# Writing out TensorE's order and the engine of each flexible task as two strings, in place of rules that decide them while the program is built

## The chip, the cores and the metric

The kernel runs on one core of one Trainium2 chip. The metric is device time in microseconds; the time before is the median of three runs. A core has a matrix engine (TensorE, PE in the profile; its weight loads are PEld), a vector engine (VectorE, DVE), a scalar engine (ScalarE, ACT), GpSimd (POOL) and SyncE (SP), which here issues DMAs. Each engine works off its own list of instructions in order; semaphores hold it where an input isn't there yet. TensorE writes to PSUM, and VectorE or ScalarE carry the result to SBUF (an eviction).

## The reference, cut to what matters

B is 8, S 3136, D 256 and d_qk 64; all inputs are float32.

```python
scores = (1 / S) * np.matmul(z, z.transpose(0, 2, 1))
attn = np.maximum(scores, 0.0) ** 2
x = u * np.matmul(attn, v)                       # stage 1
proj = x @ w_proj                                # stage 2
x1, x2, x3 = proj[..., :D], proj[..., D:2*D], proj[..., 2*D:]
x2_conv = irfft(rfft(x2, axis=1) * rfft(filter_fft, axis=0), axis=1)
out = (x1 * x2_conv * x3) @ w_out
```

## The kernel before

**Stage 1.** A batch's 3136 rows are cut into seven chunks of columns (CHUNKS: five of 512, one of 256, one of 320) and 25 tiles of 128 rows. A unit is a pair of row tiles against one chunk. Its scores (`score_mm`, task kind S) contract over only 64 rows, so the array is used in halves (64x128) or, next to spectrum work, in quarters (64x64). Relu runs on ScalarE from PSUM into R_t (line 1852), the square on VectorE (line 1861) or ScalarE (line 1859) into A_t in bf16, and the product with v (`weigh`, kind W, full array) sums into the two PSUM banks ps_o. As the scores are symmetric, some squares are transposed by DMA into the tiles M_t, M2e_t and M2o_t and used a second time. When a chunk is complete, VectorE multiplies the sum by the transposed u into xT_t (line 1903).

**Stage 2.** `add_proj` projects each finished chunk (kind A, in the last batch partly Z): gates x1*x3 (line 1217), and x2 through the first step of a Fourier transform written as matmuls (`dft1`), whose result goes to a scratch in DRAM (s_t to spec). When a batch's scratch is complete, `add_spectrum` loads it and runs the quarter-array steps forward and inverse (kind Q), with the multiplication by the filter's transform H on VectorE between (line 1307); the result goes to a second scratch. `add_end` (kind B, or Z for chunks that are put back to the end) loads that, finishes the transform, multiplies by the gates (line 1401), applies w_out and stores.

**PSUM.** Two banks hold the sums ps_o; six banks form three pairs ps_s. S and Q take a whole pair, A, B and Z one bank of a pair, of which at most three may be held at a time.

**The planner.** The program's order is not the order in which the Python code is written. Every piece of work is a `Task` with its cost on each engine that may run it, its dependencies and the buffers it takes. `Plan.go` steps through a clock of its own: it asks `pick_pe` for TensorE's next task and `pick` for each other engine's, takes the one that can begin first and emits its instructions. TensorE's tasks wait in queues by kind (S, Q, W, FA, FB, FZ); S and W leave theirs in order, Q within the first four, the F kinds within the first six. `pick_pe` chooses the kind by rules: stay with S while it is in a run of them, how much W must be in hand, whether a Q joins the run, a credit that balances W against projections. The numbers of the rules stand in RULES, one line for each 50 us of the planner's clock. Tasks that may run on either of two engines (evictions by `copy`, squares) are offered to both, and `pick` gives a task to its second engine only if it would end earlier there, with a term `give` for tasks that can't move. `fill` puts a matmul of the identity on TensorE where it would be idle near the end.

The relus run on ScalarE alone, the products with gates and with H on VectorE alone. Three queues issue DMAs: SyncE (scratch, transposes, stores), GpSimd (loads with a cast, some stores), and ScalarE (a few at the very start and end).

Of the kernel before, what the change touches and what calls it, by code (L numbers as in the profile page):

```python
# [37 lines left out]
MOST = 3  # L38
REACH = 2
Rule = namedtuple("Rule", "backlog ample stay first lead pace full give")  # L40
STEP = 50.0
RULES = [
    Rule(1.25, 5.0, 0.05, 0.5, 1, 0.5, 3.0, 1.0),
    Rule(1.25, 5.0, 0.05, 0.5, 1, 0.5, 3.0, 1.0),
    Rule(1.25, 5.0, 0.05, 0.5, 1, 0.45, 3.0, 1.0),
    Rule(1.25, 5.0, 0.05, 0.5, 1, 0.45, 3.0, 1.0),
    Rule(1.25, 5.0, 0.05, 0.5, 1, 0.45, 3.0, 1.0),
    Rule(1.25, 5.0, 0.05, 0.5, 1, 0.5, 3.0, 1.0),
    Rule(1.25, 5.0, 0.05, 0, 1, 0.55, 3.0, 1.0),
    Rule(1.25, 5.0, 0.05, 0.5, 1, 0.5, 3.0, 1.0),  # L50
    Rule(1.25, 5.0, 0.05, 0.5, 1, 0.5, 3.0, 1.0),
    Rule(1.25, 6.0, 0.05, 0.5, 1, 0.5, 3.0, 1.0),
    Rule(1.25, 6.0, 0.05, 0.5, 1, 0.5, 3.0, 1.0),
    Rule(1.25, 5.0, 0.05, 0.5, 1, 0.5, 3.0, 1.0),
    Rule(0.5, 6.0, 0.05, 0, 0, 0.4, 99, 0.5),
    Rule(0.5, 6.0, 0.05, 0, 0, 0.4, 99, 0.5),
    Rule(0.5, 6.0, 0.05, 0, 0, 0.4, 99, 0.5),
    Rule(1.25, 5.0, 0.1, 1, 1, 0.5, 3.5, 1.0),
    Rule(1.75, 99.0, 0.3, 0.5, 1, 0.55, 4.0, 1.0),
    Rule(1.25, 5.0, 0.05, 0.5, 1, 0.5, 3.0, 0),  # L60
    Rule(1.25, 5.0, 0.3, 0.5, 1, 0.6, 3.0, 1.0),
    Rule(1.25, 5.0, 0.05, 0.5, 1, 0.5, 3.0, 0),
]
SHARE = {0: 1, 2: 3}

# [117 lines left out]
class Task:  # L183


    def __init__(self, emit, cost, deps=(), takes=(), prio=0, lat=None, moves=0.0, late=0.0):
        self.emit, self.cost, self.takes, self.prio = emit, cost, list(takes), prio
        self.lat, self.moves, self.late = lat, moves, late
        self.deps = [d if isinstance(d, tuple) else (d, None) for d in deps]
        self.kids, self.frees = [], []  # L190
        self.left = len(self.deps)
        self.ready = 0.0
        self.end = None
        self.holders = 1
        for d, _ in self.deps:
            d.kids.append(self)
# [9 lines left out]
class Plan:  # L206


    def __init__(self):
# [3 lines left out]
        self.credit = 0.0  # L213
        self.mode = None
        self.quarters = False
        self.quad_run = self.score_run = 0
        self.soon = False
        self.n = 0
# [4 lines left out]
    def add(self, task, kind=None):  # L223
        task.kind = kind
        task.no = self.n
        self.n += 1
        if kind:
# [56 lines left out]
    def backlog(self):  # L284
        left = 0.0
        for w in self.queues["W"]:
            if w.source is not None and w.source.end is None:
                break
            left += w.cost["PE"]
        return left  # L290

    def queued(self, t):
        some = {id(x): x for e in ("ACT", "DVE") for x in self.pend[e] if x.ready <= t + 0.3}
        return sum(max(0.0, self.free[e] - t) for e in ("ACT", "DVE")) + sum(min(x.cost.values()) for x in some.values())

    def rule(self, t):
        return RULES[min(int(t / STEP), len(RULES) - 1)]

    def pick_pe(self):
        t = self.free["PE"]  # L300
        now = self.rule(t)
        got = {}
        for k, window in (("S", 1), ("Q", 4), ("W", 1), ("FA", 6), ("FB", 6), ("FZ", 6)):
            best = None
            for task in self.queues[k][:window]:
                s = max(t, self.ready_at(task))
                if s < INF and (best is None or s < best[0] - 1e-9):
                    best = (s, task)
            if best:
                got[k] = best  # L310
        if not got:
            return None
        more = self.queues["S"]
        quad = got.pop("Q", None)
        if self.mode == "S" and self.quarters and quad and quad[0] <= t + now.stay:
            if not more or self.quad_run < 1 and self.score_run >= now.lead:
                return (*quad, "Q")
        if more and not more[0].left:
            left = self.backlog()
            if self.mode == "S":  # L320
                if "S" in got and got["S"][0] <= t + now.stay:
                    return (*got["S"], "S")
                got.pop("S", None)
                if self.quarters and quad and quad[0] <= t + now.stay and self.quad_run < 1:
                    return (*quad, "Q")
            else:
                want = 3 if left > now.ample else 2
                free = self.pairs.when(min(want, len(more)) - 1)
                first = quad and quad[0] <= t + 0.3 and left > now.first
                if "S" in got and free > t + 0.04:  # L330
                    rest = {k: v for k, v in got.items() if k != "S" and (k == "W" or left > now.backlog)}
                    if rest and min(v[0] for v in rest.values()) < free:
                        got = rest
                    elif free < INF:
                        if first and not now.lead:
                            return max(quad[0], free), quad[1], "Q"
                        self.soon = bool(first)
                        return max(got["S"][0], free), got["S"][1], "S"
                elif "S" in got:
                    if first and not now.lead:  # L340
                        return (*quad, "Q")
                    self.soon = bool(first)
        elif quad:
            got["Q"] = quad
        if not got and quad:
            return (*quad, "Q")
        if not got:
            return None
        near = t + 0.04
        order = ["S", "Q"]  # L350
        order += ["FA", "FB", "W", "FZ"] if self.credit > 0 and self.queued(t) < now.full else ["W", "FA", "FB", "FZ"]
        for k in order:
            if k in got and got[k][0] <= near:
                return (*got[k], k)
        k = min(got, key=lambda k: (got[k][0], order.index(k)))
        return (*got[k], k)

    def pick(self, e):
        t = self.free[e]
        best = None  # L360
        for task in self.pend[e]:
            s = max(t, self.ready_at(task))
            if s == INF:
                continue
            first = next(iter(task.cost))
            if e != first:
                behind = sum(
                    x.cost[first] for x in self.pend[first]
                    if x is not task and x.prio <= task.prio and next(iter(x.cost)) == first and x.ready <= s + 0.3
                )  # L370
                end = s + task.cost[e]
                held = max((end - max(x.ready, s) for x in self.pend[e] if len(x.cost) == 1 and x.ready < end), default=0.0)
                if end + self.rule(t).give * held >= max(self.free[first], task.ready) + behind + task.cost[first]:
                    continue
            key = (round(s / 0.03), task.prio, task.no)
            if best is None or key < best[0]:
# [17 lines left out]
    def go(self):  # L394
        while True:
# [13 lines left out]
            if k:  # L409
                self.queues[k].remove(task)  # L410
                half = k in ("S", "Q")
                if half != (self.mode == "S") and self.mode:
                    start += 0.096
                    self.quarters, self.quad_run, self.score_run = half and self.soon, 0, 0
                self.score_run += k == "S"
                if k == "Q":
                    self.quad_run += 1
                    if self.score_run and not self.quarters:
                        start += 0.092
                    self.quarters = True  # L420
                self.mode = "S" if half else k
                if k == "W":
                    self.credit = min(self.credit + self.rule(start).pace, 2.0)
                elif k != "S":
                    self.credit = max(self.credit - task.cost["PE"], -2.0)
            self.run(task, e, start)
        left = sum(len(q) for q in self.queues.values()) + sum(len(q) for q in self.pend.values())
# [4 lines left out]
def kernel(  # L432
# [838 lines left out]
    def add_spectrum(b, puts, early=0):  # L1271
# [5 lines left out]
        homes = [l_p, l_p, gs_p, gs_p]  # L1277
        lasts = []
        behind = []
        ldb, gb = [None], [None]  # L1280
        for g in range(NJ // 2):
# [4 lines left out]
            if g % 2 == 0 and final:  # L1286
                ldb[0] = load_parts(D1[b % 2], 2 * g, 4, puts[:early], puts[early:], homes[g // 2])
# [709 lines left out]
```

## Time and profile before

| | |
|---|---|
| median of 3 runs | 985.75 us (985.3 to 986.08) |
| span of the profiled execution | 983.6 us |
| VectorE, multiplication by H, 120 of 128x1024 bf16 | 82.3 us |
| PE weight loads from v_t, 128x128, 2706 | 243.0 us |
| SyncE's hardware queue (q1), share of 16 DMA engines | 63.1% |
| GpSimd's software queue (q0), share of 16 DMA engines | 23.7% |
| HBM read and written | 90.26 MB and 53.35 MB |

The profiled execution's own time is its span; the runs are measured from outside and come out some 2 us longer. In a row of a group stand line, engine, operation, output and input tiles, shapes and count, then busy time, the mean of one in ns, and the idle time of the engine ahead of them with what ended it. In a row of the timeline stand start, duration, engine, line, operation and count, neighbours of one kind merged. A busy TensorE is not one at its peak: matmuls overlap, and their ends are modelled.

### The profile page before, as it was taken

The numbers are of one execution on the slowest core, as the hardware profiler recorded it, in microseconds if no ns is written. First come the engines' busy times: TensorE is split into PE (matmuls) and PEld (weight loads), VectorE is DVE, ScalarE is ACT, GpSimd is POOL, SyncE is SP. The second block draws the span as 40 slices with busy tenths as digits, with TensorE's granted clock in tenths as the row PEclk, the third lists the DMA queues.
The fourth block names the chain that finished last, engine by engine and source line by source line (L and its number), as shares of the span: only waits on it lengthen the run. The fifth ranks groups of instructions, "written<-read, shape, count | busy, mean of one in ns | idle before, by whom it ended". The sixth has DMA issues, their size and how long they took to land.

```text
span 983.6 us, 19551 instructions
## 1 busy us (share of the span) xinstructions
PE 946.7 (96%) x6776; PEld 470.0 (48%) x6877; DVE 832.4 (85%) x1468; ACT 855.6 (87%) x1185; POOL 204.4 (21%) x426
## 2 busy tenths in 40 slices
PE   6999999999999999999999999999999999999986
PEld 2344544455544544445444454544544454544654
DVE  8966798998788887988879998799788997888885
ACT  5988898899888998899988899799988999999773
POOL 5142311222022301213111230113202222000040
PEclk9999999999999999999999999999999999999999
DMA  9799789979899689997699888997869978896677
GB/s 166 140 175 160 144 144 172 180 131 162 179 216 187 128 159 203 192 184 144 143 210 197 167 153 175 209 192 151 157 158 205 215 137 146 178 221 135 172 209 227
DMA packets 332403, 170.32 MB, mean 173 GB/s; under 512 B 242598, under 2 KB 307942, under 8 KB 332304
## 3 DMA queue, kind: packets, MB, share of 16 engines
q1 hardware_dynamic: 302496, 132.43, 63.1%
q0 software_dynamic: 29168, 35.13, 23.7%
q10 hardware_dynamic: 640, 1.51, 0.5%
q8 instruction: 54, 0.88, 0.4%
q14 instruction: 45, 0.37, 0.1%
HBM read 90.26 MB, written 53.35 MB: 146 GB/s over the span
## 4 chain that ended last, share of the span: by engine, by line
PE 77%; DVE 10%; ACT 5%; issue 5%; DMA 1%; ACTq 0%; POOL 0%; DVEq 0%; SPq 0%; POOLq 0%
PE ps_o_t L561 45%; PE ps_s L561 32%; DVE A_t L1861 4%; ACT R_t L1852 3%; DVE xT_t L1903 1%; DVE xh L1307 1%; DVE gate_t L1217 1%; DVE yT_t L1401 1%; ACT A_t L1859 1%; DMA spec<-s_t 0%; ACT x_t L594 0%; DVE gs_t L598 0%; ACT s_t L594 0%; DMA spec<-gs_t 0%; DMA zn_t<-in_z_dram 0%
## 5 line engine op out<-in xcount | busy, mean ns | idle before, releaser
L1852 ACT ACTIVATE R_t<-ps_s 128x1024 f32<-128x1024 f32 (+4 forms) x512 | 467.0, 965 | 71.2 <-PE ps_s L561 68.0
L561 PE MATMUL ps_o_t<-A_t,v_t 128*128 128x512 bf16 (+4 forms) x2009 | 447.5, 353 | 9.7 <-issue 4.8
L1861 DVE TENSOR_TENSOR A_t<-R_t 128x1024 bf16<-128x1024 f32 (+3 forms) x311 | 342.8, 1119 | 58.9 <-ACT R_t L1852 58.3
L561 PEld LDWEIGHTS <-v_t 128*128 128x128 bf16 (+2 forms) x2870 | 249.0, 98 | 259.8 <-issue 74.5
L1859 ACT ACTIVATE A_t<-R_t 128x1024 bf16<-128x1024 f32 (+4 forms) x185 | 186.5, 1018 | 1.2
L561 PE MATMUL ps_s<-zT_t 64*128 64x512 bf16 (+4 forms) x1512 | 169.9, 357 | 1.6 <-DVE zT_t L598 0.5
L644 POOL COPY tick<-xT_t 1x1 bf16<-1x1 bf16 x54 | 17.9, 331 | 693.7 <-DVE xT_t L1903 693.7
L561 PE MATMUL ps_s<-xT_t,wp 128*128 128x512 bf16 (+2 forms) x412 | 101.1, 351 | 3.6 <-ACT R_t L1852 0.9
L561 PEld LDWEIGHTS <-zT_t 64*64 64x64 bf16 (+1 forms) x1545 | 52.6, 101 | 101.7 <-issue 85.8
L594 ACT ACTIVATE x_t<-ps_s 128x512 bf16<-128x512 f32 (+2 forms) x152 | 82.2, 583 | 16.0 <-PE ps_s L561 12.1
L1903 DVE SCALAR_TENSOR_TENSOR xT_t<-ps_o_t,uT_t 128x256 bf16<-128x256 f32 (+2 forms) x224 | 76.1, 383 | 10.8 <-PE ps_o_t L561 8.6
L1307 DVE TENSOR_TENSOR xh<-xh,H 128x1024 bf16<-128x1024 bf16 x120 | 82.3, 686 | 0.8
L561 PE MATMUL ps_o_t<-M_t,v_t 128*128 128x512 bf16 (+2 forms) x352 | 81.8, 353 | 0.0
L1217 DVE TENSOR_TENSOR gate_t<-ps_s,x_t 128x256 bf16<-128x256 f32 (+2 forms) x214 | 71.0, 384 | 12.5 <-PE ps_s L561 10.7
L1401 DVE TENSOR_TENSOR yT_t<-ps_s,gate_t 128x512 bf16<-128x512 f32 (+2 forms) x98 | 58.4, 626 | 11.1 <-PE ps_s L561 10.1
L561 PEld LDWEIGHTS <-wp 128*128 128x128 bf16 x448 | 42.6, 98 | 45.6 <-issue 10.3
L635 POOL DMA_DIRECT2D un_t<-in_u_dram x112 | 60.1, 561 | 5.3 <-issue 4.5
L654 POOL DMA_DIRECT2D v_t<-in_v_dram x112 | 59.6, 557 | 4.8 <-DMA v_t<-in_v_dram 1.9
L598 DVE CAST xh<-ps_s 128x512 bf16<-128x512 f32 x62 | 41.8, 687 | 18.6 <-PE ps_s L561 17.7
L561 PE MATMUL ps_s<-wp,xT_t 128*128 128x256 bf16 x398 | 56.6, 273 | 0.2
L561 PE MATMUL ps_s<-wo,yT_t 128*128 128x256 bf16 (+1 forms) x338 | 49.8, 273 | 0.7 <-ACT R_t L1852 0.4
L594 ACT ACTIVATE s_t<-ps_s 128x512 bf16<-128x512 f32 (+1 forms) x82 | 46.9, 593 | 1.8 <-issue 0.9
(165 smaller groups left out, 840.9 us busy)
## 6 DMA issues: line engine op xcount, KB each, us to landing
out_dram<-ost_t SPq DMA_DIRECT2D x60, 256.0 KB
spec<-s_t SPq DMA_DIRECT2D x96, 128.0 KB
spec_in_t<-spec SPq DMA_DIRECT2D x56, 192.0 KB
spec<-gs_t SPq DMA_DIRECT2D x56, 192.0 KB
v_t<-in_v_dram POOLq DMA_DIRECT2D x80, 128.0 KB, 4.8
un_t<-in_u_dram POOLq DMA_DIRECT2D x80, 128.0 KB, 5.4
conv_in_t<-spec SPq DMA_DIRECT2D x34, 256.0 KB
out_dram<-ost_t SPq DMA_DIRECT2D x18, 128.0 KB
```

Of the source, the lines that this page charges most:

```text
L561: wrote(nc.tensor.matmul(o, *args, **kw), o)
L594: got = nc.scalar.activation(out_, in_, AF.Copy)
L598: got = nc.vector.tensor_copy(out_, in_)
L635: nc.gpsimd.dma_start(out=t[ds(j * N1, N1), lo - t0 : hi - t0, :], in_=x[:, n2 : n2 + hi - lo, :])
L654: nc.gpsimd.dma_start(out=t[ds(j * N1, N1), ds(v_at(a), (b - a) * D)], in_=r[:, n2 + a - lo : n2 + b - lo, :].rearrange("p t d -> p (t d)"),)
L1217: got = nc.vector.tensor_tensor(g[:, ::-1] if h == 0 else g, p, x, ALU.mult)
L1307: nc.vector.tensor_tensor(x[:, 1 - i], x[:, 0], h, ALU.mult)
L1401: got = nc.vector.tensor_tensor(yb["y"][:, dh, 0:w], p, gates[b, c, dh][:, 0:w], ALU.mult)
L1852: has_read(nc.scalar.activation(blocks(box["R"], n, cw)[:rows], p, AF.Relu), p)
L1859: nc.scalar.activation(a, r, AF.Square)
L1861: nc.vector.tensor_tensor(a, r, r, ALU.mult)
L1903: nc.vector.scalar_tensor_tensor(x, f, inv_s2, ut, ALU.mult, ALU.mult)
```

## The change

RULES, the functions that read them (`backlog`, `queued`, `rule`) and the choices in `pick_pe` and `pick` go. Two strings take their place. ORDER has one letter for each task of TensorE: `pick_pe` takes the next letter and then, within that kind's queue, the task that can begin first; TensorE waits for it even if another kind could begin. ENGINES has one letter (a for ScalarE, d for VectorE) for each task that may run on either engine, in the order in which the tasks are created; `go` strikes the other engine from the task before the clock starts. When each engine's tasks run is still decided by the planner's clock. `fill` stays. Whether a run of S and Q uses quarters is now read ahead in the string.

Beside this a weight task may be split by rows and run on the half array (letters w and v, functions `weigh_rows`, `by_rows` and the task `second`); ORDER has neither letter. `weigh_short` goes through `by_rows`, which adds a wait only when the rows of one sum change; in `weigh_short` they don't. In the last batch the two spectrum loads that go into gs buffers also wait until the last inverse of the batch before has been issued (`after_q`).

```diff
-RULES = [
-    Rule(1.25, 5.0, 0.05, 0.5, 1, 0.5, 3.0, 1.0),
...
+ORDER = (
+    "ASSWBAWSSWAWSASSWSWWSSSWSWSSWWSSSWWWWSWWWWSSSWWWWASSAAWASAAWSAAWWWWWSSWWWWSSBWAWAAAWAWAAWBWSSSWWAWWS"
...
+    "AWSQWQSAAWWWWSSSWWWAWWQSSWWWWWSSSWAWWWWWWAWWWZZAAZAAZZBBBZZBBBZZBBZZZZZZQBQBZBBBQQQQQQQQBQQQQQZQZZZZ"
+    "ZZZZZZZBZZZZZZZBZBBBBBBBBBBBBBBBBBBBBBBBBBBBB"
+)
+ENGINES = (
+    "aaddddddddaadddddaaaddddaaddadadadddaadaadaaadaaaadddddddddddaaddadaaadadaddaaadaaadaddaddadaaadddaa"
...
+    "daaaaaaaaaaaadadddaaaaa"
+)
+KINDS = {"A": "FA", "B": "FB", "Z": "FZ", "w": "W"}
...
     def pick_pe(self):
...
+        if self.at == len(ORDER):
             return None
...
+        t, k = self.free["PE"], ORDER[self.at]
...
+        queue = KINDS.get(k, k)
+        best, seen = None, set()
+        for task in self.queues[queue][: {"S": 1, "W": 1, "Q": 4}.get(queue, 6)]:
...
+            s = max(t, self.ready_at(task))
+            if s < INF and (best is None or s < best[0] - 1e-9):
+                best = (s, task)
+        return best and (*best, k)
...
     def go(self):
+        either = [t for t in self.tasks if t.kind is None and len(t.cost) > 1]
+        assert len(either) == len(ENGINES)
+        for task, e in zip(either, ENGINES):
+            e = {"a": "ACT", "d": "DVE", "p": "POOL"}[e]
+            for x in task.cost:
+                if x != e and task in self.pend[x]:
+                    self.pend[x].remove(task)
+            task.cost = {e: task.cost[e]}
...
+            if not half:
+                self.quarters = False
+            elif self.mode != "S":
+                run = ORDER[self.at :]
+                self.quarters = "Q" in run[: len(run) - len(run.lstrip("SQwv"))]
...
             if g % 2 == 0 and final:
-                ldb[0] = load_parts(D1[b % 2], 2 * g, 4, puts[:early], puts[early:], homes[g // 2])
+                after_q = [(before[-1], ISSUED)] if before and homes[g // 2] is gs_p else []
+                ldb[0] = load_parts(D1[b % 2], 2 * g, 4, [*puts[:early], *after_q], puts[early:], homes[g // 2])
```

More of the change, by code (lines that the diff above doesn't have):

```diff
@@ L1 @@
-from collections import namedtuple
 from contextlib import ExitStack
@@ L38 @@
 MOST = 3
+TURN = 0.235
 REACH = 2
-Rule = namedtuple("Rule", "backlog ample stay first lead pace full give")
-STEP = 50.0
-RULES = [
-    Rule(1.25, 5.0, 0.05, 0.5, 1, 0.5, 3.0, 1.0),
[L44 to L63, printed above, removed]
@@ L194, in __init__ @@
         self.holders = 1
+        self.second, self.split, self.flips, self.flip = None, False, False, None
         for d, _ in self.deps:
@@ L212, in __init__ @@
         self.pend = {e: [] for e in ("ACT", "DVE", "SP", "POOL")}
-        self.credit = 0.0
         self.mode = None
         self.quarters = False
-        self.quad_run = self.score_run = 0
-        self.soon = False
-        self.n = 0
+        self.flip, self.parted, self.turned = None, True, 0.0
+        self.rest = []
+        self.n = self.at = 0
+        self.tasks = []
         self.spare = []
@@ L226, in add @@
         self.n += 1
+        self.tasks.append(task)
         if kind:
@@ L282, in run @@
                 self.offer(kid)
[L284 to L297, printed above, removed]
@@ L299, in pick_pe @@
-    def pick_pe(self):
[L300 to L311, printed above, removed]
-            return None
[L313 to L356, printed above, removed]
@@ new lines, in pick_pe @@
+    def pick_pe(self):
+        if self.at == len(ORDER):
+            return None
+        t, k = self.free["PE"], ORDER[self.at]
+        if k == "v":
+            s = max(t, self.ready_at(self.rest[0])) if self.rest else INF
+            return (s, self.rest[0], k) if s < INF else None
+        queue = KINDS.get(k, k)
+        best, seen = None, set()
+        for task in self.queues[queue][: {"S": 1, "W": 1, "Q": 4}.get(queue, 6)]:
+            mine = {id(s) for s in task.takes[1:]} if k == "Q" else set()
+            if mine & seen:
+                continue
+            seen |= mine
+            s = max(t, self.ready_at(task))
+            if s < INF and (best is None or s < best[0] - 1e-9):
+                best = (s, task)
+        return best and (*best, k)
@@ L362, in pick @@
             s = max(t, self.ready_at(task))
[L363 to L376, printed above, removed]
+            key = (round(s / 0.03), task.prio, task.no) if s < INF else None
+            if key and (best is None or key < best[0]):
                 best = (key, s, task)
@@ L408, in go @@
                 continue
[L409 to L425, printed above, removed]
+            if not k:
+                self.run(task, e, start)
+                continue
@@ new lines, in go @@
+            (self.rest if k == "v" else self.queues[KINDS.get(k, k)]).remove(task)
+            rows = k == "w" and task.second is not None
+            half = k in "SQv" or rows
+            if self.mode and half != (self.mode == "S"):
+                start += 0.096
+                self.flip, self.parted = None, True
+            if not half:
[3 more added lines that the diff above has]
+                self.quarters = "Q" in run[: len(run) - len(run.lstrip("SQwv"))]
@@ new lines, in go @@
+            if k in "SQ":
+                self.parted = True
+                if task.flips:
+                    self.flip, self.parted, self.turned = 0, False, start + task.cost["PE"]
+            elif half:
+                if rows:
+                    task.cost["PE"] /= 2
+                    task.split, task.flip = True, self.flip or 0
+                    task.second.flip = task.flip ^ 1
+                    self.rest.append(task.second)
+                elif self.flip not in (None, task.flip):
+                    start = max(start, self.turned + TURN)
+                self.flip, self.parted, self.turned = task.flip, False, start + task.cost["PE"]
@@ L426, in go @@
+            self.mode = "S" if half else "W"
+            self.at += 1
             self.run(task, e, start)
+            if k in "Ww" and task.second is not None and not rows:
+                task.second.cost["PE"] = 0.0
+                self.run(task.second, e, self.free["PE"])
         left = sum(len(q) for q in self.queues.values()) + sum(len(q) for q in self.pend.values())
@@ L1277, in add_spectrum @@
         homes = [l_p, l_p, gs_p, gs_p]
+        before = list(inverses)
         lasts = []
@@ L1671, in score_mm, with block, laid, by_rows @@
         live[un] = ps
-    acc, full = {}, {}
+    acc, full, row_sums = {}, {}, {}
+    def block(un, i, at):
+        b, c, k = un
+        cw = CHUNKS[c]
+        kind, pair = plans[b, c][k]
+        if kind == "S":
+            return live[un][at, ds(i * cw, cw)]
+        a = home[pair[i]]
+        m, nb = mirrors[b, a, c], pair[i] - tiles[a][0]
+        if c == NC - 1:
+            return m[at, ds(nb * cw, cw)]
+        return m[at, 0 : len(tiles[a]) * cw].rearrange("p (i n j) -> p i n j", n=len(tiles[a]), j=P)[:, :, nb, :]
+    def laid(un, o):
+        b, c, k = un
+        return o.rearrange("p (i j) -> p i j", j=P) if plans[b, c][k][0] == "M" and c < NC - 1 else o
+    def by_rows(dh, h, *args, **kw):
+        other, last = row_sums.get(dh, (h, None))
+        if other != h:
+            tc.add_manual_dep(
+                nc.tensor.nop().ins, last.ins.name, mybir.DependencyInfo(needs, reason.DATA),
+                reason="the other rows' sum",
+            )
+        row_sums[dh] = h, nc.tensor.matmul(*args, **kw)
+    def weigh_rows(un, flip):
+        b, c, k = un
+        cw = CHUNKS[c]
+        for i, t in enumerate(plans[b, c][k][1]):
+            if t == NT - 1:
+                continue
+            p = N1 if plan.quarters else P
+            for m in range(0, P, p):
+                for h in range(2):
+                    dh, at = h ^ flip, slice(h * N1, (h + 1) * N1)
+                    by_rows(
+                        dh, h, laid(un, acc[dh][ds(m, p), :cw]), row(v16[b], t)[at, ds(dh * P + m, p)], block(un, i, at),
+                        start=False, stop=False,
+                    )
     w_first, w_last = {}, {}
@@ L1685, in weigh @@
                     continue
-                o = acc[dh][:, :cw]
-                if kind == "S":
-                    x = live[un][:, ds(i * cw, cw)]
-                else:
-                    a, nb = home[t], t - tiles[home[t]][0]
-                    m = mirrors[b, a, c]
-                    if c == NC - 1:
-                        x = m[:, ds(nb * cw, cw)]
-                    else:
-                        n = len(tiles[a])
-                        x = m[:, 0 : n * cw].rearrange("p (i n j) -> p i n j", n=n, j=P)[:, :, nb, :]
-                        o = o.rearrange("p (i j) -> p i j", j=P)
+                x, o = block(un, i, slice(0, P)), laid(un, acc[dh][:, :cw])
                 matmul(
@@ L1716, in part @@
             t = pe(
-                "W", lambda: weigh(un, dhs), c_pe(*[cw] * (n * len(dhs))), deps,
-                [ps_o[dh].slots for dh in dhs] if k == 0 else [],
+                "W", lambda: weigh_rows(un, t.flip) if t.split else weigh(un, dhs), c_pe(*[cw] * (n * len(dhs))),
+                deps, [ps_o[dh].slots for dh in dhs] if k == 0 else [],
             )
             t.source = src
+            after_it = t
+            if len(dhs) == 2:
+                t.second = after_it = Task(
+                    lambda e: weigh_rows(un, t.flip ^ 1) if t.split else None, {"PE": c_pe(*[cw] * n)}, [(t, ISSUED)]
+                )
+                after_it.kind, after_it.no = "V", t.no
             if b == 0 and c == 0:
@@ L1723, in part @@
             if 1 in dhs:
-                done(t)
+                done(after_it)
             if k == 0:
@@ L1727, in part @@
                     w_first[dh] = t, i_
-            w_last.update({dh: t for dh in dhs})
-            return t
+            w_last.update({dh: after_it for dh in dhs})
+            return after_it
         k, n = un[2], global_k
@@ L1810, in weigh_short @@
                 n = N1 if plan.quarters else P
-                matmul(
-                    acc[dh][ds(m, n), :cw], row(v16[b], NT - 1)[h, ds(dh * P + m, n)], live[un][h, ds(i * cw, cw)],
+                by_rows(
+                    dh, dh, acc[dh][ds(m, n), :cw], row(v16[b], NT - 1)[h, ds(dh * P + m, n)], live[un][h, ds(i * cw, cw)],
                     start=False, stop=False,
@@ L1837 @@
         st = pe("S", sg, sum(costs) + extra, deps, [pair_slots] * len(g))
+        st.flips = bool(more)
         tails[gi] = st
```

31 lines of the change are left out of this document (added).

## The prediction

> **What bounds the kernel now.** I read the page first (busy shares and the chain), then the sums by stretch, then TensorE's own timeline, then the groups by form.
>
> ```profile
> span 983.6 us, 19551 instructions
> PE 946.7 (96%) x6776; PEld 470.0 (48%) x6877; DVE 832.4 (85%) x1468; ACT 855.6 (87%) x1185; POOL 204.4 (21%) x426
> PE 77%; DVE 10%; ACT 5%; issue 5%; DMA 1%; ACTq 0%; POOL 0%; DVEq 0%; SPq 0%; POOLq 0%
> ```
>
> The span is 983.6 us and the median of the runs 985.75: 2.15 us lie around the span, and I add them back at the end. TensorE is busy for 96% of the span and carries 77% of the chain. So the question is what TensorE does with its time, not how busy the others are. The sums by stretch (span, busy of PE, PEld, DVE, ACT and POOL, granted clock, DMA) say where it is idle:
>
> ```profile
> 0.00:40.00 40.00, 30.48 (x155) 11.94 (x159) 35.02 (x78) 29.56 (x35) 15.94 (x40) 1.00 0.92 154
> 40.00:920.00 880.00, 866.19 (x6125) 426.51 (x6221) 750.53 (x1299) 789.41 (x1082) 176.27 (x363) 1.00 0.88 171
> 920.00:983.60 63.60, 50.03 (x498) 31.56 (x498) 46.81 (x94) 36.66 (x70) 12.24 (x23) 0.97 0.76 218
> ```
>
> Idle TensorE: 9.5 us in the first 40, 13.8 in the 880 of the body, 13.6 in the last 63.6. These three numbers are nearly all that a better order can win; the clock is full, but for 0.97 at the end. They shrink further:
>
> ```profile
> 4.81 0.61 PE L564 MATMUL ps_s<-ident,xT_t 128*128 128x128 bf16 x4 [4.81 <-ACT xT_t L594]
> 5.94 1.03 PE L561 MATMUL ps_s<-zT_t 64*128 64x512 bf16 x4 [0.52 <-DVE zT_t L598]
> ...
> 975.86 0.38 PE L561 MATMUL ps_s<-wo,yT_t 128*128 128x256 bf16 x2
> ```
>
> At the start 4.8 us pass before there is anything to multiply, so the head has 9.5 - 4.8 = 4.7 to win. TensorE's last matmul ends at 975.86 + 0.38 = 976.2; the 7.4 us behind it are copies and stores, so the tail has 13.6 - 7.4 = 6.2. There TensorE also runs filler matmuls that compute nothing:
>
> ```profile
> L561 PE MATMUL ps_s<-ident 128*128 128x512 bf16 x19 | 5.1, 381 | 0.0
> 951.18 1.04 PE L561 MATMUL ps_s<-ident 128*128 128x512 bf16 x4
> ```
>
> 19 of them, 5.1 us: disguised waiting. Of the body's 13.8 a part is no waiting at all. The page has 6877 weight loads but only 6776 matmuls: 101 records are missing. How much hole one leaves is read from the timeline of the body:
>
> ```profile
> 503.57 0.38 PE L561 MATMUL ps_o_t<-A_t,v_t 128*128 128x512 bf16 x1
> 504.01 1.89 PE L561 MATMUL ps_o_t<-A_t,v_t 128*128 128x512 bf16 x8
> 320.30 1.02 PE L561 MATMUL ps_o_t<-M_t,v_t 128*128 128x512 bf16 x4
> 321.26 0.41 PE L561 MATMUL ps_s<-zT_t 64*64 64x512 bf16 x4
> 321.50 0.39 PE L561 MATMUL ps_s<-xh,TZ 64*64 64x512 bf16 x4
> 321.82 2.55 PE L561 MATMUL ps_o_t<-A_t,v_t 128*128 128x512 bf16 x11
> ```
>
> One matmul of 512 columns shows 0.38 us, eight in a row 1.89: they follow each other every (1.89 - 0.38) / 7 = 0.216 us. A missing record thus opens a hole of 2 x 0.216 - 0.38 = 0.05 us, about 5 us for 101. Real waiting in the body is about 13.8 - 5 = 9 us in 880.
>
> The same rows hold the price that matters for this change. Four full-array matmuls start at 320.30; without a break the next would start at 320.30 + 4 x 0.216 = 321.16, but the quarter-array matmuls of the score start at 321.26: 0.10 us lost. Going back, 321.50 + 0.216 = 321.72 and the next starts at 321.82: 0.10 again. So **each change between full-array work (weights, projections, outputs) and half- or quarter-array work (scores, spectrum) costs about 0.095 us** and is hidden inside "busy". Counted over the whole trace from the matmuls' forms there are 506 such changes, from 4.81 / 5.94 above to the last one here:
>
> ```profile
> 956.97 0.41 PE L561 MATMUL ps_s<-R_t,TZ 64*64 64x256 bf16 x8
> 957.31 0.39 PE L561 MATMUL ps_o_t<-xT_t,wp 128*128 128x512 bf16 x1
> ```
>
> That is 48 us of the span, more than all idle time together.
>
> **The change, part by part.**
>
> *The order string.* ORDER holds 2245 letters: 928 W, 512 S, 408 A, 222 B, 136 Q, 39 Z, the same tasks that the planner of before places. So no matmul appears or goes, and the streaming time stays. What changes is how often S and Q (partial array) stand between the others (full array). Counting letters, ORDER has 274 unbroken stretches of S and Q; the tasks in the order of before have 248 (a few changes of the trace's 506 lie inside other tasks, such as the tables' transposes). 26 stretches more are 52 changes more: 52 x 0.095 = **+4.9 us, certain**, since TensorE sits on the path almost everywhere. 42 of them fall in the first four of the eight batches. The Trainium skill, "TensorEngine Tiling (Array Packing)", Key Properties, says that a change of tiling mode drains the array, which speaks against this order; from the drain of about 128 cycles at 2.4 GHz in "TensorE: Matmul & The Clock Gate", the phase DRAIN, 0.053 us for each is an estimate, and the sum would be +2.8. The trace shows nearly twice that, and the trace's price is used.
>
> *What the shorter stretches may buy.* A stretch of three S or Q tasks takes all three PSUM pairs, and projections and outputs (A, B, Z), which need half a pair, then wait until a relu or an eviction gives one back:
>
> ```profile
> L1852 ACT ACTIVATE R_t<-ps_s 128x1024 f32<-128x1024 f32 x408 | 402.5, 1038 | 62.7 <-PE ps_s L561 59.9 <-DVE A_t L1861 1.2
> ```
>
> One relu is 1.04 us, and all of them run on ScalarE one after another; that group also waits 62.7 us for scores. Before, 149 stretches hold three tasks (SQS 74, SSS 62, QSS 11, two others); in ORDER it is 125 (SSS 56, QSS 21, SQS 20, SSQ 17, eleven others), and single and double stretches rise. So ScalarE is fed more evenly and PSUM is less often full. The trace cannot price that; the bounds are nothing recovered (0) and all idle of the body (13.8). The row nearest to real waiting is the corrected 9 us; I take two thirds of it, **-6**, because the list can be arranged around each wait, while late transfers stay outside its reach.
>
> *The engine string.* 1223 tasks may run on either engine. Matched with the tasks in the order in which the program creates them, evictions on VectorE go from 239 to 301 (+62) and squares on ScalarE from 192 to 228 (+36). Durations:
>
> ```profile
> L1861 DVE TENSOR_TENSOR A_t<-R_t 128x1024 bf16<-128x1024 f32 x238 | 287.3, 1220 | 46.8 <-ACT R_t L1852 46.3
> L1859 ACT ACTIVATE A_t<-R_t 128x1024 bf16<-128x1024 f32 x154 | 164.6, 1080 | 1.0
> L594 ACT ACTIVATE x_t<-ps_s 128x512 bf16<-128x512 f32 x128 | 73.6, 615 | 12.8 <-PE ps_s L561 10.2 <-DVE x_t L598 1.0 <-DVE gate_t L1217 1.0
> L598 DVE CAST x_t<-ps_s 128x512 bf16<-128x512 f32 x44 | 29.4, 686 | 4.6 <-PE ps_s L561 3.8 <-ACT x_t L594 0.4
> ```
>
> ScalarE: -62 x 0.615 + 36 x 1.080 = +0.8 us; VectorE: +62 x 0.686 - 36 x 1.220 = -1.4. The loads stay at 87% and 85%, hidden under TensorE; the direct cost is 0. If that cover were gone, +0.8 would be the whole price.
>
> *Head.* 4.7 us to win at most, 0 at least; the first batch gets 14 more changes, already counted. Half is my value, **-2.4**: what it waits for there is the loading of z and the first squares, and only the second of these yields to order.
>
> *Tail.* From 920 on the chain runs through two DMA steps and then through VectorE:
>
> ```profile
> 931.81 4.63 DMA spec<-s_t
> 936.49 2.87 DMA spec_in_t<-spec
> ...
> 951.39 0.60 DVE M2e_t L598
> 952.00 0.60 DVE xh L1307
> ```
>
> The two transfers, 7.5 us, are not changed by any order. Behind them VectorE alternates multiplies and evictions of 0.6 us; of the last batch's spectrum evictions 7 stand on VectorE before and 4 in ENGINES, which takes up to 3 x 0.6 = 1.8 us off that chain. With a little of the filler time I take **-2.4** (bounds: 0, and 6.2 + 5.1 = 11.3). The tail's work itself is the same: 112 letters behind the last S in both orders, 39 ahead of the first Q.
>
> *The added wait.* In the last batch two loads of spectrum parts into the gs buffers now also wait until the batch before has issued its last inverse. That inverse has to give back its gs buffer ahead of them anyhow, so the cost is 0; at most it is one load late, the 2.87 us above. It is issued from SyncE, and what would be late next are stores behind it in the same queue. The rest of the diff (splitting a weight task by rows, letters w and v) has no letter in ORDER and issues nothing.
>
> Sum: +4.9 - 6 - 2.4 - 2.4 = -5.9 us. 983.6 - 5.9 = 977.7 for the span, + 2.15 = **979.9 us**.
>
> **The rivals.**
>
> 1. *The idle time isn't there for an order to take, and the switches are paid in full* (slower). Place: the body, above all batches one to four with 42 of the 52 extra changes. Price +4.9. For it: the body has only 9 us of real waiting in 880, and an order that is shortest when it never switches has little left to gain. Against: the head and the tail yield something without any switch. It decides as soon as less than 2.9 us is recovered in all; with the tail's 1.8 alone: 985.75 + 4.9 - 1.8 = 988.9.
> 2. *A wash*: the shorter stretches recover about what they cost, between 3 and 7 us. For it: the two terms have the same origin, as each added change is there to fill a hole of its own size. Time about 985.5.
> 3. *Nearly all waiting goes*: 9 in the body, 4 in the head, 5 in the tail, minus 4.9, is -13: 972.7. For it: the PSUM argument holds everywhere at once. Against: the waits in the body include late transfers, which a list made beforehand can't see.
>
> **How the numbers follow.** Forecast (3 to 10 us faster) 0.53; rival 3 0.12; rival 2 0.15; rival 1 0.20. About 0.2%, 2 us, is what a measurement of this kernel can tell from no change. Faster 0.53 + 0.12 = 0.65, same 0.15, slower 0.20. The range leaves out about a tenth at each end: 973 (most of rival 3's gain) to 989.5 (the switches in full and the tail's gain lost in part). The forecast's own range is 975.5 to 983.
>
> **What would show it.** Right: about 558 changes between full and partial array; TensorE idle in the body down from 13.8 to 8 or less (the 5 of missing records stay); the wait of the relus for scores under 62.7; fewer than 19 fillers; ScalarE and VectorE busy within 2 us of 855.6 and 832.4. Wrong: idle in the body still near 13.8 with the 52 changes there (rival 1); changes at another price than 0.095; or one new wait of some microseconds on a load or on the last batch's spectrum, because TensorE now keeps a fixed order and everything behind a late input stands still.

## The result and the profile after

The changed kernel takes 977.57 us (median of 4 runs, 976.98 to 981.28) against 985.52 for the kernel before in the same session: a ratio of 0.9916 with a 95% interval from 0.9892 to 0.994, 8 us faster. Two later repeats of the changed kernel gave 0.9915 [0.989, 0.9939] and 0.9903 [0.987, 0.9936]. The prediction was 979.9 us.

The page of the changed kernel, with the lines that answer to those shown of before:

```profile
span 975.3 us, 19343 instructions
PE 942.9 (97%) x6664; PEld 468.5 (48%) x6765; DVE 830.5 (85%) x1492; ACT 859.5 (88%) x1161; POOL 201.0 (21%) x426
PE 89%; DVE 4%; ACT 2%; DMA 2%; issue 2%; SPq 0%; ACTq 0%; DVEq 0%
```

The chain of the work that ended last now runs through TensorE for 89% of the span (77% before); VectorE's and ScalarE's shares went from 15% to 6%. That is the first sign that TensorE waits less for squares and relus. The sums by stretch of the same kernel:

```profile
0.00:40.00 40.00, 30.07 (x153) 11.30 (x157) 33.34 (x70) 28.72 (x37) 15.74 (x40) 1.00 0.98 144
40.00:920.00 880.00, 871.15 (x6078) 430.71 (x6173) 753.44 (x1333) 800.10 (x1066) 173.04 (x363) 1.00 0.89 172
920.00:975.30 55.30, 41.70 (x436) 26.46 (x437) 43.75 (x91) 30.64 (x59) 12.26 (x23) 0.95 0.77 231
```

Idle TensorE is 9.9 us in the head (9.5 before), 8.9 in the body (13.8), 13.6 in the tail (13.6). So the idle rows show 5 us of the 8.3 that the span lost, all of it in the body. Both profiles lack about a hundred matmul records, each of which opens some false idle time; more on that below. The view of who waited for whom (total us, times, longest), first of before, then of the changed kernel:

```profile
DVE A_t L1861 <- ACT R_t L1852: 58.3, 56, 2.4
ACT R_t L1852 <- PE ps_s L561: 68.0, 84, 4.2
```

```profile
DVE A_t L1882 <- ACT R_t L1873: 27.1, 42, 2.3
ACT R_t L1873 <- PE ps_s L540: 50.9, 76, 2.7
```

The fillers of the changed kernel, in the groups by form from 920 us on:

```profile
L540 PE MATMUL ps_s<-ident 128*128 128x512 bf16 x7 | 2.0, 380 | 0.0
```

The squares on VectorE wait half as long for relus, the relus less for scores, and of the 19 fillers 7 are left. (There are also fewer squares on VectorE than before.)

**Where the time went.** The idle rows hide most of it. A matmul of 512 columns is drawn 0.38 us long, and the next one may start 0.216 us after this one's start; a pause of up to 0.163 us between two matmuls therefore leaves no idle time in the profile at all, and a longer one shows without its first 0.163. (Where full and partial array change, 0.095 us of these 0.163 go to the change, and only 0.068 of a pause stay hidden.) In the timeline of before:

```profile
83.55 0.59 PE L561 MATMUL ps_o_t<-A_t,v_t 128*128 128x512 bf16 x2
84.13 0.61 PE L561 MATMUL ps_o_t<-M2e_t,v_t 128*128 128x512 bf16 x2
84.57 0.59 PE L561 MATMUL ps_s<-xT_t,wp 128*128 128x512 bf16 x2
```

Two matmuls start at 83.55, so the next should start at 83.55 + 0.43 = 83.98. It starts at 84.13: 0.15 us lost, and no idle time is drawn. I therefore counted pauses from the starts: from one start to the next, less the columns of the first at 0.4218 ns each (0.216 us for 512), less 0.095 us where full and partial array change, with missing records put back in from the program's own list of matmuls. To compare the same work in both programs I also took the time from the 41st to the last score unit (a unit is a group of score matmuls that start together; the 41st stands near 72 us). Pauses over 0.04 us between 40 and 915 us, and the changes there:

| | before | changed |
|---|---|---|
| pauses of 0.04 to 0.163 us | 44, 4.0 us | 17, 1.6 us |
| pauses over 0.163 us | 27, 8.4 us | 3, 0.8 us |
| changes of full and partial array | 464 | 510 |
| 41st to last score unit | 849.4 us | 844.1 us |

The body gained 10.1 us in pauses (12.5 to 2.4, before rounding) and paid 46 x 0.095 = 4.4 for changes: 5.7 net, and the time from the 41st to the last score unit fell by 5.3. The changed kernel's TensorE pauses over 0.163 us three times in 875 us. The rest of the 8.3 lies in head and tail: up to the 41st score unit 72.9 before and 71.9 after, from the last one to the end 61.4 and 59.3.

### The profile page after: what moved, and what is told of

It is laid out like the page before. It is cut to its first block, busy times and chain, and to the rows that moved or that the text cites. A ratio compares the mean times of both kernels' runs of the same rounds, so it can differ in the third digit from the quotient of the medians.

```text
span 975.3 us, 19343 instructions
## 1 busy us (share of the span) xinstructions
PE 942.9 (97%) x6664; PEld 468.5 (48%) x6765; DVE 830.5 (85%) x1492; ACT 859.5 (88%) x1161; POOL 201.0 (21%) x426
## 4 chain that ended last, share of the span: by engine, by line
PE 89%; DVE 4%; ACT 2%; DMA 2%; issue 2%; SPq 0%; ACTq 0%; DVEq 0%
PE ps_o_t L540 51%; PE ps_s L540 36%; ACT R_t L1873 1%; DVE A_t L1882 1%; PE ps_o_t L1681 1%; DMA conv_in_t<-spec 1%; DMA spec_in_t<-spec 1%; DVE yT_t L1382 1%; DMA M2e_t<-A_t 1%; DVE xh L1288 1%; DVE R_t L1288 0%; ACT A_t L1880 0%; DVE gate_t L1196 0%; PE ps_s L543 0%; DVE xT_t L1924 0%
## 5 line engine op out<-in xcount | busy, mean ns | idle before, releaser
L540 PE MATMUL ps_o_t<-A_t,v_t 128*128 128x512 bf16 (+2 forms) x1936 | 441.4, 354 | 10.8 <-issue 4.4
L540 PEld LDWEIGHTS <-v_t 128*128 128x128 bf16 x2706 | 242.8, 98 | 255.2 <-issue 76.9
L1882 DVE TENSOR_TENSOR A_t<-R_t 128x1024 bf16<-128x1024 f32 (+2 forms) x274 | 300.4, 1112 | 30.4 <-ACT R_t L1873 27.1
L1880 ACT ACTIVATE A_t<-R_t 128x1024 bf16<-128x1024 f32 (+4 forms) x222 | 222.3, 1019 | 1.9 <-DMA M2e_t<-A_t 0.9
L540 PE MATMUL ps_s<-zT_t 64*128 64x512 bf16 (+5 forms) x1418 | 161.9, 356 | 1.9 <-DVE zT_t L577 0.5
L623 POOL COPY tick<-xT_t 1x1 bf16<-1x1 bf16 x54 | 14.7, 272 | 688.3 <-DVE xT_t L1924 688.3
L540 PE MATMUL ps_s<-xT_t,wp 128*128 128x512 bf16 (+2 forms) x411 | 104.5, 352 | 1.1 <-DVE gate_t L1196 0.5
L573 ACT ACTIVATE x_t<-ps_s 128x512 bf16<-128x512 f32 (+2 forms) x126 | 71.8, 587 | 16.5 <-PE ps_s L540 14.7
L577 DVE CAST x_t<-ps_s 128x512 bf16<-128x512 f32 (+2 forms) x85 | 52.2, 623 | 12.3 <-PE ps_s L540 6.5
L614 POOL DMA_DIRECT2D un_t<-in_u_dram x112 | 59.9, 557 | 7.6 <-issue 5.7
L540 PE MATMUL ps_s<-wo,yT_t 128*128 128x256 bf16 (+1 forms) x360 | 54.3, 273 | 0.3 <-DVE yT_t L1382 0.2
```

The costliest lines, as they stand in the source:

```text
L540: wrote(nc.tensor.matmul(o, *args, **kw), o)
L573: got = nc.scalar.activation(out_, in_, AF.Copy)
L577: got = nc.vector.tensor_copy(out_, in_)
L614: nc.gpsimd.dma_start(out=t[ds(j * N1, N1), lo - t0 : hi - t0, :], in_=x[:, n2 : n2 + hi - lo, :])
L1880: nc.scalar.activation(a, r, AF.Square)
L1882: nc.vector.tensor_tensor(a, r, r, ALU.mult)
```

## The experiments

**The control: the changed code with the strings of before.**

```diff
-ORDER, ENGINES = (those of the change)
+ORDER, ENGINES = (the order and engines that the rules of before arrive at, written out)
```

> The changed kernel's code with the strings of before: the order and the engines that the rules of before arrive at, written out. If all of the gain comes from what stands in the strings: the time of before, ratio 1.000 within 0.003. If the rest of the diff (the wait of the two last spectrum loads, quarters read ahead, sums by rows) matters: a ratio under 0.997 or over 1.003.

Measured: 986.66 us, ratio 0.999 [0.9974, 1.0006]. So the rest of the diff is worth nothing that can be measured; the strings carry the gain.

The profile of e5 is of the slowest of its ten runs, 990.67 us, and shows how far two executions of one order can lie apart. TensorE's matmuls stand in it in the order of before, but for three fillers fewer. Yet the body has 17.8 us of pauses, and 854.6 us pass from the 41st to the last score unit, against 12.5 and 849.4 in the profile of before. One place makes most of the difference:

```profile
119.91 2.30 DVE L1883 TENSOR_TENSOR A_t<-R_t 128x640 bf16<-128x640 f32 x3 [5.67 <-issue]
120.79 0.70 PE L541 MATMUL ps_o_t<-A_t,v_t 128*128 128x320 bf16 x4 [2.95 <-DVE A_t L1883]
```

VectorE waits 5.67 us ahead of these squares, for nothing that the profile shows, and TensorE 2.95 us behind it; the pauses here make 4.1 of the 17.8 us. The changed order's body took 844.1 to 844.6 us in all five profiles that have it (the first one, e4, e7, e8, e11). So the 5.3 us of the body are a comparison with an execution of before that had no such wait.

**One string at a time.** In e1 `pick` of before, with its rules, chooses engines under the new ORDER; in e2 `pick_pe` of before chooses the order under the new ENGINES. The part of e1's edit that takes the string out (RULES and `pick` of before, which come back, are left out here; e2 is the kernel before with these lines put in):

```diff
 def go(self):
-    either = [t for t in self.tasks if t.kind is None and len(t.cost) > 1]
...
-        task.cost = {e: task.cost[e]}
```

> ORDER as in the changed kernel; the engine of each flexible task is chosen again by the rules of before. If the gain lies in TensorE's order and the engine choice only has to be sensible: 978 to 981.5 us, pauses of TensorE in the body about as in the changed kernel. If order and engines only work as a pair: 984 us or more, with TensorE idle in the body (40 to 915 us) back above 13 us.

> The kernel before, its order by rules, with the engine string of the changed kernel. By the prediction's step (engine loads change by +0.8 and -1.4 us, hidden): 984 to 987 us. If the engines carry the gain: 981 us or less. If the string is worth nothing without the order it was found with: 988 us or more.

Measured: e1 1000.12 us, ratio 1.013 [1.0097, 1.0162]; e2 1065.05 us, 1.0782 [1.075, 1.0814]. Neither string is worth anything alone, and the engine string under another order costs 78 us. Part of what e1 lacks stands in its waits; the squares of VectorE in the groups by line:

```profile
L1914 DVE TENSOR_TENSOR A_t<-R_t 128x1024 bf16<-128x1024 f32 (+2 forms) x306 | 336.1, 1114 | 69.1 <-ACT R_t L1905 67.1 <-DMA M2e_t<-A_t 0.8
```

VectorE waits 67.1 us for relus, where the changed kernel has 27.1. That relus stand behind other work on ScalarE more often under the rules' engines would explain it, but I have not shown it. e1's pauses in the body are 82 of together 23.2 us, over before's 12.5. For e1 the second expectation came true in its time (984 or more); its sign, TensorE idle above 13 us, was missed at 875 - 863.19 = 11.8. For e2 the last one came true (988 or more), far beyond its bound.

**Forty small disturbances in each string.** In e3 40 pairs of score tasks of the body are parted by the weight task that follows; in e6 40 neighbouring letters of the engine string change places.

```diff
-ORDER:   ASSW
+ORDER:   ASWS
-ENGINES: ad
+ENGINES: da
```

(One place of 40 in each string.)

> The changed kernel; at 40 places of the body a pair of score tasks is parted by the weight task that follows it (SSW becomes SWS), 80 more changes between full and partial array, each task moved by one place. If shorter stretches feed ScalarE more evenly in general, as the prediction has it, only the changes are paid: 80 x 0.095 = 7.6, 985 us (983.5 to 987). If the gain is a fit of each place to its neighbours, waits come back on top: 990 us or more, with pauses of TensorE in the body rising by more than 5 us.

> The changed kernel; at 40 places of the body two neighbouring letters of the engine string are exchanged (a d becomes d a), 80 tasks move, no engine's load changes. By the prediction's step (only loads count, and they are hidden): within 2 us of the changed kernel in the same call. If each letter is fitted to its place, as the 40 exchanges in the order string were (waits in the body up by about 9 us): 5 to 20 us more than the changed kernel.

Measured: e3 1001.13 us, 1.0129 [1.0105, 1.0154]; e6 996.81 us, 1.0084 [1.0056, 1.0112]; the changed kernel beside e6 978.17 (e7). Moving 40 tasks of 2245 by one place costs 22 us against e4 (979.06 beside it, below), which differs from the changed kernel in the tail alone; the changes explain 7.6 of it. Exchanging 80 of 1223 engine letters, with as many letters for each engine as before (busy times within 2.3 us of e7's), costs 18.6 against e7.

Not all of this comes from the exchanged places. Up to 120 us in e3 and 144 us in e6 the three engines run the same lists as in the changed kernel; yet the 41st score unit came at 75.3 and 75.0 us, and at 70.6 in e7. The changed order itself had it anywhere from 70.4 to 75.7 us in its five profiles. From the 41st to the last score unit e3 takes 862.0 us and e6 858.5, against 844.5 in e7: 17.5 and 14.0 us are what the exchanges cost there.

The longest of TensorE's waits in the body of e6, then the only one of the changed kernel beside it (e7):

```profile
PE ps_s L541 <- ACT R_t L1874: 3.4, 6, 1.4
PE ps_s L541 <- DVE x_t L578: 1.9, 3, 0.9
PE ps_s L541 <- ACT x_t L574: 1.2, 3, 0.5
```

```profile
PE ps_s L540 <- DMA spec_in_t<-spec: 0.9, 1, 0.9
```

and the same stretch of e7 in the sums by stretch:

```profile
40.00:915.00 875.00, 874.09 (x6135) 426.94 (x6134) 749.17 (x1326) 795.92 (x1061) 173.08 (x363) 1.00 0.90 172
```

In e7 TensorE's body has one visible wait, 0.9 us for a load; in e6 PSUM banks come back late from relus (ps_s waiting for R_t: no matmul among these reads R_t), and evictions into x_t come late, some as the release of a bank and some as the input of the matmul that waits. In e3 the pauses of the body rise from 2.4 to 11.4 us; these 9 and the 7.6 for changes make 16.6 of its 17.5. Had shorter stretches helped by themselves, e3 would have been 985. Both experiments came out as expected for a fit of each place to its neighbours.

> The changed kernel once more, to stand beside the others of this call: ratio 0.9916 within 0.002.

Measured: 0.9915 [0.989, 0.9939], as expected.

**The tail's evictions.** The 32 spectrum evictions of the last batch get their engines of before back (9 letters).

```diff
-"aaaadaaaaaaaadaaaaaaaadaaaaadaaa"
+"adaaaaadaaaaadaaadadaaaaadaaaaad"
```

> The changed kernel; the 32 spectrum evictions of the last batch run on the engines that they had before (7 instead of 4 on VectorE, 9 letters differ). By the prediction's tail step: 3 x 0.6 = 1.8 us more, 979.4 us. If the tail waits for its DMAs or for TensorE anyway: 977.6 us, within 0.5.

> The kernel of e4 once more, beside the changed kernel in the same call. If three evictions fewer on VectorE in the tail are worth 1.8 us: 1.8 us over e7. If the tail waits for something else: within 0.5 us of e7.

Measured: e4 979.06 us, ratio 0.9915 [0.9889, 0.9941]; e8 981.22, ratio 0.9929 [0.9902, 0.9957], beside 978.17 and 0.9915 for e7. From the last score unit to the end: 61.5 and 60.6 us with the letters of before, 59.3, 61.0 and 58.8 in three profiles of the changed kernel. The effect has the expected sign and lies within the spread of one kernel; it is not settled. These nine letters also bring back ten of the 12 fillers that had gone (17 in e4 and e8). `fill` puts them where the planner's clock expects TensorE to be idle, so their number tells what the planner expects more than what TensorE waits for on the chip.

**Are the added changes needed?** Two pairs of strings of my own, found by a short search from the strings of before, judged by the planner's clock alone: e9 never with more than 248 stretches of S and Q, e10 free, ending at 286.

```diff
-ORDER = (274 stretches of S and Q)
+ORDER = (e9: 248 stretches; e10: 286)
-ENGINES = (those of the change)
+ENGINES = (348 letters of before changed in e9, 320 in e10)
```

> Two strings of my own, found by a short search from the strings of before with the kernel's own planner as the judge, under the condition that the order never has more than the 248 stretches of S and Q of before; 149 of them hold three tasks, as before. If shorter stretches are what takes the waits away, as the prediction has it: within 1.5 us of before. If the waits go because order and engines are fitted to each other, and the added changes are by-products: 3 to 6 us faster than before, waits of TensorE in the body (over 0.04 us, 12.5 us before) at 4 to 8.

> The same search without that condition; it ended with 286 stretches (76 changes more than before), 130 of them with three tasks. If shorter stretches are what helps: clearly faster than e9. If they are by-products that cost 0.095 us each: waits lower than in e9 by about the 7 us that the changes cost, time within 1.5 us of e9.

> The changed kernel beside the two: ratio 0.9916 within 0.002.

Measured: e9 990.34 us, 1.0033 [1.0016, 1.005]; e10 990.83, 1.0034 [1.0012, 1.0055]; e11 977.35, 0.9903 [0.987, 0.9936]. By the planner's own clock both were about 6 us shorter than the strings of before; on the chip both are 3 us longer. (The clock ends at 974.3 us with the strings of before, 967.8 with e9's, 968.6 with e10's and 960.9 with those of the change; of these last 13 us the chip gave 8.) For e9 neither branch of its expectation held. For e10 the second did: 0.5 us from e9, with 6.4 us less of pauses. The count of pauses, and how far it explains the body:

| 40 to 915 us | pauses over 0.04 us | changes | 41st to last score unit |
|---|---|---|---|
| before | 12.5 us | 464 | 849.4 us |
| changed (e7) | 2.7 us | 511 | 844.5 us |
| e9 | 15.0 us | 462 | 852.1 us |
| e10 | 8.6 us | 522 | 851.6 us |

e9 has 2.5 us more pauses than before and as many changes: 2.7 us longer. e10 saves 3.9 in pauses and pays 58 x 0.095 = 5.5 for changes: 1.6 expected, 2.2 measured. The changed kernel saves 9.8 and pays 4.5: 5.3 expected, 4.9 measured. So pauses and changes at 0.095 us account for the body within 0.6 us. Each row is one execution, and e10's is its fastest (985.49 us, where the median is 990.83): its row explains the body of that execution, and not the 3 us of the median. Whether a pair of strings with fewer changes could remove as many pauses stays open: my search was too short, and what it gained on the planner's clock the chip did not give.

## Why the prediction was right

The forecast was 5.9 us and the gain 8.0. Beneath the sum the match is weaker. The body was forecast at +4.9 - 6 = -1.1 net and came out at -5.3; head and tail were forecast at -4.8 together and came out at -3.1, within the spread of one kernel. An error one way offset an error the other way, so that the sum came this near is in part luck.

**The price of the changes** held. 44 more in the whole trace (506 to 550; 52 were forecast from the strings), and by the medians of the four kinds of transition in the changed kernel each costs 0.093 to 0.103 us: +4.2 against +4.9. The estimate of 0.053 from the drain in the Trainium skill's "TensorE: Matmul & The Clock Gate", phase DRAIN, is too small here. That a change drains the array (the Trainium skill, "TensorEngine Tiling (Array Packing)", Key Properties) fits the time lost at each change; the drain itself is not seen in the trace.

**The body** was mis-sized: -6 forecast, -10.1 measured. The step that failed is "Real waiting in the body is about 13.8 - 5 = 9 us". It took the bound from idle time, which leaves out the first 0.163 us of every pause; counted from the starts there were 12.5 us to win, and the strings won four fifths. A second error partly cancelled this one: missing records opened more than 5 us of false idle time. The changed kernel shows 875 - 866.20 = 8.8 us idle between 40 and 915 in the profile that lacks 101 records, and 0.9 in e7's, which lacks none:

```profile
40.00:915.00 875.00, 866.20 (x6040) 427.39 (x6134) 749.92 (x1327) 797.02 (x1061) 173.04 (x363) 1.00 0.89 172
```

So each missing record leaves about 7.9 / 94 = 0.08 us rather than 0.05, and of the 13.8 us idle in the profile of before, which lacks 96 records between 40 and 915 us, some 8 are false and some 6 real. For the same reason the sign "idle 8 or less" was missed at 8.9, although nearly all real waiting had gone. The sign for the relus came true: 45.2 us for scores in that group (the prediction's 62.7 is the group's whole idle time; 59.9 of it was for scores).

**The reason given for the body** does not hold as a general one. "ScalarE is fed more evenly and PSUM is less often full" because stretches are shorter: e3 has 40 stretches more than the changed kernel, and shorter ones, and its pauses rise by 9 us; e10 has 12 more and keeps 8.6 us of pauses. That a shorter stretch helps in its place is not excluded, since e10, found like e9 but with 38 stretches more, has 6.4 us less of pauses than e9. What the runs do show is that order and engines must fit each other: wherever one was altered without the other, the body grew from 844.5 us (862.9 in e1, 922.9 in e2, 862.0 in e3, 858.5 in e6). Which property of a fitted pair keeps them away stays open.

**The engine string at 0** was right in its sum and wrong in its meaning. Loads stayed (VectorE 832.4 to 830.5, ScalarE 855.6 to 859.5, the latter 2 us beyond the forecast's 2), but e6 shows that letters that hardly move load are worth 14 us in the body (18.6 in the whole time). The prediction treated an engine's load as what an assignment costs; e6's waits point to the moment at which a relu or an eviction is done and gives back its PSUM bank.

**The head**, -2.4 forecast, is not shown to have gained: 71.9 us to the 41st score unit in the first profile, 70.6 in e7, 75.7 in e11, against 72.9 in the profile of before and 73.3 in e5. There a new wait came, as the prediction's last part feared, though neither on a load nor on the spectrum. The chain of the changed kernel has this piece, and its timeline these two rows:

```profile
24.51 4.99 DMA M2e_t<-A_t
```

```profile
29.60 1.23 DVE L1882 TENSOR_TENSOR A_t<-R_t 128x1024 bf16<-128x1024 f32 x1 [2.29 <-DMA M2e_t<-A_t]
31.63 0.59 PE L540 MATMUL ps_o_t<-A_t,v_t 128*128 128x512 bf16 x2 [1.96 <-DVE xT_t L1924]
```

A transposing DMA out of a square's buffer takes 4.99 us; the next square that needs the buffer waits 2.29. The multiplication into xT_t stands behind that square on VectorE, and TensorE waits 1.96 for it. No such row stands among the waits of before. It varies between executions, and so do the times of one kernel: in e11 the body took 844.5 us as in e7, the head 5 us more and the tail 2 us less.

**The tail**, -2.4 forecast: 61.4 to 59.3, 61.0 and 58.8 us, 12 fillers fewer. In the right direction, about the right size, its cause (three evictions fewer on VectorE) left open by e4 and e8.

**The added wait** of the spectrum loads cost nothing (e5).

Rival 1 fell: far more than 2.9 us was recovered. Rival 2 fell too: the pauses won, 10.1 us, are twice what the changes cost. Rival 3 had the body right ("nearly all waiting goes") and took head and tail too large.

## What to carry to other kernels

Where TensorE is busy nearly all the time, count its lost time from the starts of its matmuls, not from idle rows: here 12.5 us of pauses stood against about 6 us of idle time that was real. An order and an assignment that fit each other are one object: disturbing 40 places of either, or keeping only one half, cost 18 to 86 us in all, and at least 14 in the body. It is to be feared, though no run here shows it, that another edit of such a kernel (a buffer, a duration, a DMA) spoils the fit as well. One profile of a kernel can hold a wait that another lacks: the strings of before took 849.4 us of body in one execution and 854.6 in another. A search judged by a model should end on the chip: 6 us won on the planner's clock by a short one were none here.

## What the runs showed of the hardware beyond that

A change between full-array and partial-array matmuls costs 0.093 to 0.105 us in either direction (medians of each kind of change in thirteen profiles), some 52 us of this kernel's 975. A transposing DMA of one square's buffer took 5.0 us on the chain in the head, and the square that needed the buffer next waited for its end. The head of one and the same program took 70.6 us in one execution (e7) and 75.7 in another (e11), while the 844.5 us of the body came out alike to 0.1 us. In the second, TensorE was busy less, and the granted clock (the last figure but two) fell to 0.83; e7's row, then e11's:

```profile
30.00:40.00 10.00, 9.64 (x53) 4.13 (x54) 10.00 (x14) 7.88 (x10) 2.47 (x5) 1.00 0.67 93
30.00:40.00 10.00, 8.04 (x33) 2.53 (x31) 8.19 (x11) 6.76 (x7) 2.48 (x5) 0.83 0.67 105
```
